# Attention and two mixer blocks on one core: float32 weight copies leave DRAM, Strassen sums are built from high and low parts, and the work gets a new order

## The chip, the cores and the metric

The kernel runs on one core of one Trainium2 chip. The metric is device time in microseconds (us) of one launch, lower is better. A core has a matrix engine (TensorE, PE in the profile, with its weight loads as PEld), a vector engine (DVE), a scalar engine (ACT), GpSimd (POOL) and an engine that issues DMA transfers (SP). Each runs its own queue of instructions in order and waits on semaphores.

## The reference, cut to what matters

```python
# q, k, v: (4, 12, 448, 64), float32; x: (4, 448, 768)
scores = cap * tanh((q @ k.T) / sqrt(64) / cap)
attn   = exp(scores - max); attn = attn / (sum(attn) + 1e-9)
x  = heads_to_columns(attn @ v)
# block 1
theta = x @ w_theta
y  = w_tok_r @ (x * cos(theta)) + w_tok_i @ (x * sin(theta))
u  = x + y
x  = u + relu(u @ w_ch)
# block 2
u  = x + (relu(x.T @ w_tok1) @ w_tok2).T
out = u + relu(u @ w_ch1) @ w_ch2          # 768 -> 1536 -> 768
```

All of it is float32. The kernel keeps that precision by splitting an operand into a high part in the float32r format and a low part (the rest), and adding three matmuls (high x high, high x low, low x high).

## The kernel before

**Stages.** The four batches are done as two pairs. First attention of all batches (`attn`), then, woven with the rest of attention, block 1 and block 2 of batches 0 and 1 (`token(0, ...)`, `rest(0)`), with plain products of 128 columns; then `token(1, ...)` and `rest(1)` for batches 2 and 3. For the second pair every product of block 1's theta, of `w_ch`, of `w_ch1` and of `w_ch2` is done by a Strassen-like scheme of seven products for eight (`fast`, `fast2`), two batches at a time. It needs, beside three quarters of a weight as they are, four sums of its quarters, `s1` to `s4`; they are made in `combine` and split again into high and low parts (tiles `F` in float32, `S` or `w` split).

**Weights.** Weights come in as float64, a pair of 32-bit words for each number (`raw`). `convert` builds the float32 value (`cw`) with ACT, DVE and POOL, splits it into `hl`, and writes the split to DRAM (`cu`, `ct`, `ca`, `cb`); for all weights of index 6 to 35 it also writes the float32 value itself to DRAM (`f6` to `f35`, dictionary `whole`). Where the second pair needs the sums, `combine` loads quarters of these float32 copies (`F<-f`); only for the first six weights it gets them by adding a high and a low part on DVE (`F<-w`). `RE`, `FE` and `SL` say which engine does which addition (v is DVE, p is POOL).

**Attention.** For each pair of heads and each chunk of keys, `scores` makes a matmul into a two-bank PSUM tile `sp`, ACT does tanh and exp into a tile `t` (three buffers, tag `t`; `tm` for the shared tail chunk), and `av` multiplies by the values. At the end of a pair of heads `finish` copies the result from PSUM to `xr` (two buffers), sends the sums through small DMAs (`pk`, `sr`, `dn`) to invert and spread them, multiplies `xr` by `dn`, and for batches 2 and 3 stores `xr` in DRAM (`xd`). A buffer of `xr` is free when that store has landed.

**Order.** All of this is recorded as operations and then put in order by a list scheduler (`Plan.schedule`). It takes the ready operation with the lowest priority number, and the table `RANKS` adds a shift to the priority of each operation. `SB` and `PS` give the number of buffers of each tag; a buffer is handed out in the order of recording.

Of the kernel before, what the change touches and what calls it, by code (L numbers as in the profile page):

```python
# [95 lines left out]
!s5aq>?{*P#S$S@yE250<wAIfxPFxoZfh7qTqJ}anuYKnbw0Z#gx?<yp=Hq!dQ}LaC-JK#Luhb&2(222aPF}X=H48_=*L4iUn7J@Q93-{C4~I+v6-
?R<iE~%MXw6spP?aKHIO#Y@mBs2wiF7XGX1rj9zwo3A?%{x>lv?hgAk_94B@4}LRk9_^>$KrGK9-dhww*M2wz+X;b@N#exXgicSBf}ZRJyrK*zZdj-3eM-
SZ(llNrKm86n(2xTI7F&mIloz=043(NDL7Av{c*!!4nK?`KAY@KnA;;tJ9msMG9h2utX<6K&6)3Sl+zTIv@jJ)3wnG<0H|M~;P1=#oUD6ytRz%%tABGa(f
DH-
s{LCys}3ZLLIN6m9B3`(w~Fmo`7r|8~CTP(Kq|E~39JN$N8G)ubzvevtI%)G5YyDf(RWPYC7H1m;*B+M3W;1?E(pzTc;O7W8ZmA@rUd!k9vd#7@e4QGOeB  # L100
-%2DB*;NyXpXqNO^}0aU7Ur^dZwL|X=TUEC@kFBMK4>8nWQ>xz5{ZkUvu43W;#T6*)G0*WhxUZ<3AELtpRJ5Lk+Sm4HKwl;q!%*oW#s=vUTMbb$-
dM$1PxIL^O?()v|B~_O8V-(J%mHh@dor%DMp<#i9~D0-
b0;n)alMR<4JE~J#JwBwdrRid2CyVNN*$Ej`okPhrYj=SMEe&9&3LowAP{B7{(~Z_gUJ{C2p5Lkyu9Dh&|}0_2O*RW4!y>hky94Oj-
ZKtSxJHp1E|S>~TVyf32^I^gECI*9h&H+g|csq`W6#D}6r6{Dwi(LTKtjn-WilkVT!IjPn!osYu>av>Ohcvss^4>E~1EUPil`wCh3L#hm-
=D67i++SBJq`tDDDF518OKq9e%dV4uD^=aFkwe3Q^(X4$9!n#xle>281(Rj?x<39Fd9R1xym`43hT5tN?PrZ@*IdjzgG7cew^&P@G{Ru6n=CVfY`ySHy8z
d5eF@9iO=F@&P;a$Slj5m?9((189BF~Nx?%vAxpPWV3Xdq)Z`cER!m$|)6of3>wc^hj^yAsT$HT0ijKJy9Z`R>fv!|1;Vw6x|dbfsMf#;ixWFEl(sXb#N-
nEOWhszm!M2|YMJ+ZnqcbL>O^|J@Qo-HqI9*6<|h`q1&*Zq{iR^ub>q<lOwgm>)6LE3`jNpM&Wm$;IhR+>yKg4)f?p{r;@QJ*;PCLSfp>pwCO0OK;ZnQOX
x_UT%WE>CoR8y0@^t^XYE^v>c$$leB-7@4nDikG3DFY*7fevhE$A>mtVMun8XU6YW^HkAH@DiEiqzg0}A&V-?}ht?6*>ckDBBzmz_^LQ6-
&2i&J87^@cdv;<|RIkUN-AwTQWit&pwPEGD=Ue=-1Wr;+7+Kwm8V?O(!cN1YSYy2j2sL344Fy`&7L#Z_(jG+H=zr%~xv7SrdhwRTm&Tw5qRcL&Nb=X-
rk=V-kX9=A+(@zoq$vLXW7-OL29OH~4{|fT+K-b@-  # L110
n^Crs@v3n~dXay+ZU_(1XV35HpEWr~S$WRqd}#lK?@i33Cv$5;+?aWOPCx&F)>52@afHLH=}zi)Sq8sm4ZqWUU|*^*)=SKxKjj1AeJ{W_hcMoygvQiaPk-
OiZYz9aDSfVho>IEY(6>r!N_;NU#x6&BNz#Yt^GV_sti@NfeUkX%Cfq6L?RvoO>^VX{#ymjS&N%%zXYW(5t<E^>JCyQ1(7k~0EPX9too<58lf)BQyAk9Sr
cNo^-@-fwow7BXO<%QHPmV#jl>CpW-
;D3A&{UYvk9L&^Z<GHZeIKE$D(Uv*?d5x<co})K33WspWd%4twJ2LoXhxsq8UGH_6<C{pDSMH44}E`6URC;efj*vv7T9!nmhuwheRIL)l#l+FQ-
2EUGK%m4XRtJNzdUbwk`v;m6Iq9C%&7_AgTz;#Hoo~AVGZ>*vsY7~aV_Z<)E`dWeC*vS`YA+zH|ngB--
>h*`sl^@HN>xIQw$o)=1n9t_cPF)i#>UmbYNa7`Z$|mcX=n{zDN7fgr4*_iM$(VJCO31*srC~-jy-VQLhqxFJ|lm;^&Na3w7?|thAu*8u;IC#;Hi#<Iu}B
3w8Le#rM8Fb}v65?_u)pqyFWzolO`>KiAN2amJp`cLCzfjC+*$8P>J(MTvygvkP^m(Dqa4+eleg@j=eeamuE02m5}FoMnzj;Cn47YY06fnd?btU&MG9==%
=RZ_+j|<wFPq=&vkg>xg?ZuP&J;3l0&clK%v4c1jjd_dd#QA^w3rPH+!K^L>yy6GapGDd_l`{d$e`ounTizZdPNO4cxs8<>aYvx+sik9b<1MB*pr@;dcz(
AXE*`g}^+$MoHov+*3|llguoHktap?t9vJOBd2V(*JqNYm(QTyIY(5G0^lldHrcy9U9Ih4NI*dd`9`L^tF`wqba`xI-
jG?P|}x^-jZd!X)QF}O&=@LCZDGg*GSuX&L>8sgcJ1lH0e9Z`;7Z?fHgTtn?LERDQ#9$=ZllZFA9(@$UZlTY|TF58#WMbR-  # L120
fd}p^pb*<JrK@1W-IwrQS`XE0BMkudnXhF24Vw-KE4o5kJJb4ZmRbegfxRGT|EPcBO6W$Y|WlHxM~IK^vfb7yymqSc~^aFQ8px$`A6riLjLL4|&~be;xJ5
(tn3+lP!`9<>|j9WtY(J<)mv;R+aIqksd()OSD-<_>s_`I$slBBcv&xL#W1{-B14oN!RBLoQ9Ui2*deq4?T#x!1W1;#*mB9g|-
c~|AcYWTg>;nti!d;P3Prv#;i|VnDy_hc4?bu1$g9I>UWK7ot_gdd~f6XBgT4*a7i$pSqqvTrk?|9N1fI>AJjwig(Bo5io*=;A^E*@hY9~BAgaQfgl@6j_
fHAm1j9|YlgF~;tTC!dPP;v{|BL)LNMA?4#fgh*9|>nQcgn|*zL{_WIx4dE8LaOb>OM#q2c4zp`)cyaLH8Y$UqhSUpmi974I=+dzEQ!#eDWHT?nwG$!Yul
{mOefuZvY{iFqQoBPWNWM#}OYUo=@E`Nxz>q%(Fa_F2{W$|9wIg!qfEiD<Q$T*baWx8Z6cMg|54ai|ahoM+Wgn^mEc!Z%FGL(r0_gDKh$y(IvL^tgib;3=
7M-Kd+NNn7Vtl&%Q1ivMt{~5_VDlJYgQ`HsTY(=Klxviczm1-
xK&Qk+%DGkiMQEzD@Us@FD@VHHTm9q0Rk#zr^>wgsVwEN$4vXOJ7|nFDu?lC_sMU*!WU?(x|fGGvddomzB1;oFyL2x9EF{&{}6BwmU7ls*v}q&NO2mOWS#
QM}3mMf%p^F@E_7+DSw!FAL9bS6J>pUPLQ`%ciZQ3f_m4IKZ$lDg%SAPMVo6W`<A?3#Q*BvQ3oiVD8~0!#A~UypYhVMos+{ln>yos_oD1Ftu=KgP`3=<W%
&M%vWntU<gX^wBkw42O#W+x-~0}v?uTQ1ZzW8QjrXc=-L2B32Z@)GzTjuEQQF#QF0-
<YKaMB;JL&O++@eXclf2IuAC?~qQRgn56+&0i2h(<@bT4{RuUuqjwjDC~g_DNK=aAQmbmV8N9OWxxo5ObE7oGO8$n4dOJBYEG5hm$=()K-  # L130
_f88hDal)_SNs?>ySCn*J>g<KiJhAbl-n11y7hOr+De~I!eKYm16Ca~qZN@6Y{(R2&H{}1Ob)@b&LR0FGk_;klMR-
# [1533 lines left out]
```

## Time and profile before

| what | value |
| --- | --- |
| median of three runs | 919.63 us (918.73 to 920.24) |
| the profiled execution, its own time | 919.92 us |
| its span, first to last instruction | 918.0 us |
| PE busy | 901.8 us (98%) |
| DVE busy | 686.2 us (75%) |
| ACT busy | 517.8 us (56%) |
| POOL busy | 350.2 us (38%) |
| DMA traffic | 169.25 MB, mean 184 GB/s |

The busy time of an engine is the union of its instructions. Matmuls overlap, so an uninterrupted PE shows as fully busy and the time that counts there is idle time and time at a lower granted clock. In a timeline row the bracket at the end is the idle time of that engine just before the row, with the instruction that ended it. [...]

### The profile page before, as it was taken

Reading aid. Unit: us, or ns where it says so; the run is one execution under the profiler, and the core shown is the slowest. Engines: PE = TensorE matmul, PEld = TensorE weight load, DVE = VectorE, ACT = ScalarE, POOL = GpSimd, SP = SyncE. Lnnn points to the kernel's source line nnn. Section 1 sums busy time; section 2 is a strip of 40 time slices with the busy share of each in tenths; the row PEclk is TensorE's granted clock in tenths of the full one; section 3 lists DMA queues with packets and bytes.
Section 4 is the critical chain, followed back from the end, with each engine's and each line's share of the span. In section 5 each row is a group of like instructions: output and inputs, shape, how many; then the busy total and the mean of one; then the engine's idle time right before and its main releaser. Section 6 shows DMA issues by size and latency. Waiting matters only on the chain.

```text
span 918.0 us, 13715 instructions
## 1 busy us (share of the span) xinstructions
PE 901.8 (98%) x4776; PEld 697.1 (76%) x4776; DVE 686.2 (75%) x1150; ACT 517.8 (56%) x871; POOL 350.2 (38%) x298
## 2 busy tenths in 40 slices
...
GB/s 220 225 241 235 261 216 250 180 270 175 167 126 201 263 252 85 168 217 173 286 268 236 214 277 193 382 148 78 52 124 135 55 30 102 95 193 101 220 116 143
DMA packets 97708, 169.25 MB, mean 184 GB/s; under 512 B 11752, under 2 KB 79976, under 8 KB 97640
## 3 DMA queue, kind: packets, MB, share of 16 engines
...
## 4 chain that ended last, share of the span: by engine, by line
PE 61%; DVE 4%; DMA 2%; ACT 2%; issue 1%; SPq 0%; POOL 0%; ACTq 0%; DVEq 0%; POOLq 0%
PE P L551 24%; PE c L551 18%; PE t L551 6%; PE tm L551 6%; PE wc L551 3%; PE av L551 2%; PE tp L551 1%; PE xp L551 1%; DMA raw<-wt 1%; DMA raw<-wu 1%; DMA pk<-sv 1%; PE sp L551 1%; ACT t L551 1%; DVE g L551 1%; DVE cw L551 0%
## 5 line engine op out<-in xcount | busy, mean ns | idle before, releaser
L551 POOL TENSOR_TENSOR cw<-cw,raw 128x384 uint32<-128x384 uint32 (+2 forms) x94 | 95.4, 1017 | 257.0 <-DVE cw L551 147.1
L551 PE MATMUL tm<-WT,zn 128*128 128x448 f32 x504 | 115.6, 376 | 0.2 <-DVE WT L551 0.2
L551 PEld LDWEIGHTS tm<-WT,zn 128*128 128x128 f32 x504 | 92.5, 189 | 18.5 <-issue 4.7
L551 ACT ACTIVATE t<-sp,consts 128x896 f32<-128x896 f32 x72 | 72.0, 1002 | 36.6 <-POOL t L551 12.1
L551 PE MATMUL c<-g,w 128*128 128x448 f32 x432 | 89.6, 365 | 0.1
L551 PE MATMUL c<-XHL,w 128*128 128x448 f32 x432 | 89.6, 366 | 0.0
L551 PEld LDWEIGHTS c<-XHL,w 128*128 128x128 f32 x432 | 81.0, 188 | 7.2
L551 PEld LDWEIGHTS c<-g,w 128*128 128x128 f32 x432 | 80.9, 188 | 7.1 <-DVE XT L551 0.5
L551 ACT ACTIVATE t<-t,consts 128x896 f32<-128x896 f32 x72 | 74.9, 1043 | 1.7
L551 PE MATMUL P<-XHL,w 128*128 128x448 f32 x324 | 72.9, 366 | 0.0
L551 POOL TENSOR_TENSOR F<-F,F 128x384 f32<-128x384 f32 (+1 forms) x42 | 43.0, 1023 | 76.7 <-DVE F L551 58.9
L551 POOL TENSOR_TENSOR t<-t,t 128x896 f32<-128x896 f32 x24 | 52.4, 2183 | 51.3 <-ACT t L551 13.6
L551 DVE SCALAR_TENSOR_TENSOR cw<-raw,cw 128x384 uint32<-128x384 uint32 (+2 forms) x94 | 69.7, 744 | 2.4
L551 ACT CAST w<-cw 128x384 fp32r<-128x384 f32 x72 | 35.2, 507 | 57.6 <-PE c L551 25.7
L551 PE MATMUL av<-t,vt 128*64 128x448 f32 x288 | 64.8, 556 | 2.6 <-ACT t L551 2.0
L551 PEld LDWEIGHTS P<-XHL,w 128*128 128x128 f32 x324 | 60.7, 188 | 5.3
L551 POOL TENSOR_TENSOR XHL<-XT,XHL 128x448 fp32r<-128x448 f32 x30 | 38.0, 1268 | 49.9 <-ACT XHL L551 30.0
L551 DVE TENSOR_TENSOR w<-cw,w 128x384 fp32r<-128x384 f32 x72 | 45.6, 645 | 13.4 <-ACT w L551 13.3
L551 PE MATMUL th<-XHL,w 128*128 128x448 f32 x216 | 52.1, 378 | 0.6 <-DVE rc L551 0.6
L551 ACT CAST S<-F 128x384 fp32r<-128x384 f32 (+1 forms) x72 | 31.5, 460 | 36.2 <-DVE F L551 16.9
L551 DVE TENSOR_SCALAR cw<-cw 128x384 uint32<-128x384 uint32 (+2 forms) x94 | 45.2, 481 | 8.3 <-ACT cw L551 7.4
L551 PEld LDWEIGHTS th<-XHL,w 128*128 128x128 f32 x216 | 38.6, 188 | 14.3 <-issue 8.6
...
## 6 DMA issues: line engine op xcount, KB each, us to landing
...
f<-cw SPq DMA_DIRECT2D x60, 192.0 KB
...
F<-f SPq DMA_DIRECT2D x36, 192.0 KB
...
```

Source lines behind the costliest of these rows:

```text
L551: getattr(eng[o.eng], name)(*map(real, a), **{x: real(y) for x, y in k.items()})
```

## The change

1. `convert` no longer writes float32 copies; the dictionary `whole`, the 60 stores `f<-cw` and the 72 loads `F<-f` are gone.
2. `combine` makes all four quarters by adding a high and a low part. For weights 6 to 11 and 12 to 23 these are 36 more additions on DVE (128x384); for weights 24 to 35 (`mixed2`) they are 18 on DVE and 18 on POOL (128x256, `RE["d"]` is `vpvp`). The quarter that was not loaded split before is loaded now: nine loads of a split weight are 128x1536 instead of 128x2x384, and 18 loads `S<-cu` of 128x256 are new.
3. `combine` no longer raises the priority of these operations.
4. `t` tiles rotate over five places: three buffers of tag `t` and two of tag `ex`, which stand empty until the second pair.
5. `xr` has three buffers instead of two.
6. `SHIFT`, the unused bytes that are put ahead of some tiles, and `RANKS` have new numbers. `GRP` is all ones, so the loop over chunks yields as before.

```diff
+TS = ("t","t","t","ex","ex")
-SB = {..., 't': 3, ..., 'xr': 2, ..., 'ex': 2}
+SB = {..., 't': 3, ..., 'xr': 3, ..., 'ex': 2}
-RE = "vvvv"
+RE = {"t":"vvvv","w":"vvvv","c":"vvvv","d":"vpvp"}
-SHIFT = {'w': 8, 'wg': 16, 'rc': 16}
+SHIFT = {'zx': 16, 'kq': 16, 'raw': 16, 't': 16, 'w': 16, 'wg': 16}
 RANKS = r"""
-c-lpq3D}KQ*T+w$SE5qNlp#b>84`+wqB1my5}}kLDPz...
+c-l3a2i%X<`^UdVgrt;Ji6rquN+b#uQW+(Yrj?M9EhH...
...
-        if key[0] == "u" and key[1] in plain:
-            if key[1] not in whole:
-                whole[key[1]] = dram(f"f{key[1]}", P, [DM])
-            sp_.dma_start(whole[key[1]][:, key[2] * n:(key[2] + 1) * n], wv)
...
     def quad(a, c):
-        return [("c", a, full(a)), ("c", c, half(c))]
+        return [("c", a, full(a)), ("c", c, full(c))]
...
+        def next_t():
+            tag = TS[count[0] % len(TS)]
+            count[0] += 1
+            return sbuf("t", tag, [1024])[...] if tag == "ex" else sbuf("t", tag, [2, S])
...
-                t = pt[c] = sbuf("t", "t", [2, S])
+                t = pt[c] = next_t()
...
-    def combine(t, srcs, N):
-        with pri(-100):
-            for j, src in zip((2, 0, 1, 3), srcs):
-                x[j] = sbuf("F", "cw", [CW])[:, :N]
-                if isinstance(src, tuple):
-                    (pool if RE[j] == "p" else dve).tensor_tensor(out=x[j], in0=f(src[0]), in1=f(src[1]), op=ALU.add)
-                else:
-                    sp_.dma_start(x[j], src)
+    def combine(t, srcs, N, how):
+        for j, src in zip((2, 0, 1, 3), srcs):
+            x[j] = sbuf("F", "cw", [CW])[:, :N]
+            (pool if how[j] == "p" else dve).tensor_tensor(out=x[j], in0=f(src[0]), in1=f(src[1]), op=ALU.add)
...
-        combine(t, [whole[24 + g * FB + q // 3][...] for q in (...)], N)
+        i, q = divmod(2 * (e + 3), 3)
+        weight("u", 24 + g * FB + i, None, DM // CW)
+        with pri(-100):
+            for h in range(2):
+                sp_.dma_start(f(t[0][h]), cache["u", 24 + g * FB + i][:, h, N * q:N * q + N])
+        combine(t, (t[0], A["22"], A["11"], A["12"]), N, RE["d"])
```

On each engine the number of instructions changes as follows: PE 4313 and 4313, with the same kinds and shapes; DVE 54 more; POOL 18 more; ACT two table loads more (22 instead of 20); SP 114 fewer (475 instead of 589). The order changes everywhere. Counting as one form the score matmuls, the float32 and the float32r ones apart, the `av` products (of `t` and of `tm` apart), the sums, the transposes and the 128-wide products, PE's order goes from one form to another 308 times before and 276 times now.

The first place is DVE in the token stage of the first pair, where results of attention of batch 2 go to `xr` (`xr_314`, `xr_330`, `xr_360` and `xr_384` are the first four, written in turn). Before, the third copy stands a little behind the conversion of `wt1`, ahead of work on the second buffer:

```order
L551 TENSOR_SCALAR cw_475_2225<-cw_475_2225 112x256
L551 TENSOR_SCALAR cw_472_2170<-cw_472_2170 112x256
L551 SCALAR_TENSOR_TENSOR cw_472_2170<-raw_438_2008,cw_472_2170 112x256
L551 COPY xr_360_2248<-av_341_1963 128x448
L551 SCALAR_TENSOR_TENSOR cw_475_2225<-raw_469_2080,cw_475_2225 112x256
L551 TENSOR_TENSOR rc_390_2218<-rc_390_2218,XT_82 128x448
L551 TENSOR_TENSOR xr_330_1900<-xr_330_1900,dn_333_2192 128x448
```

Now there is a third buffer, and it is the fourth copy that needs the place of `xr_314`; it stands 15 rows behind the multiplication that readies `xr_314` for its store:

```order
L559 TENSOR_TENSOR xr_314_1815<-xr_314_1815,dn_317_1942 128x448
L559 TENSOR_TENSOR rc_356_1994<-rc_356_1994,XT_82 128x448
L559 SCALAR_TENSOR_TENSOR pk_332_1888<-pk_332_1888,consts_74 56x16
L559 RECIPROCAL pk_332_1888<-pk_332_1888 56x16
L559 TENSOR_TENSOR rc_356_1994<-rc_356_1994,XT_82 128x448
L559 COPY sv_361_2056<-av_341_1903 128x448
L559 TENSOR_TENSOR zn_373_2060<-tp_374_2030,zn_372_2041 128x512
L559 COPY xr_360_2071<-av_341_1903 128x448
...
L559 TENSOR_SCALAR cw_470_2095<-cw_470_2095 128x384
L559 COPY xr_384_2124<-av_359_2045 128x448
```

The third copy no longer depends on the first store, and the fourth one does.

The second place is ACT a little later, where the last pieces of `wt2` (`raw_483`, then `raw_486`) are converted between tanh and exp of batch 3 (`t_498`, then `t_502`). Before, the last piece stands directly ahead of the tanh of `t_502`:

```order
L551 ACTIVATE cw_490_2779<-raw_483_2703 128x224
L551 CAST XHL_83<-XT_82 128x448
L551 CAST ch_488_2803<-cw_487_2742 128x224
L551 ACTIVATE cw_493_2825<-raw_486_2768 128x224
L551 ACTIVATE raw_486_2768<-raw_486_2768 128x224
L551 ACTIVATE t_502_2834<-sp_501_2818,consts_74 128x896
```

Now it stands directly ahead of the tanh of `t_498`, one chunk earlier, behind all the pieces before it:

```order
L559 ACTIVATE raw_483_2668<-raw_483_2668 128x224
L559 CAST XHL_83<-XT_82 128x448
L559 CAST ch_485_2749<-cw_484_2629 128x224
L559 CAST ch_488_2755<-cw_487_2706 128x224
L559 ACTIVATE raw_486_2715<-raw_486_2715 128x224
L559 ACTIVATE cw_493_2772<-raw_486_2715 128x224
L559 ACTIVATE t_498_2789<-sp_497_2774,consts_74 128x896
```

On SP the load of `raw_486` stands as the fifth row behind that of `raw_480`, where it was the 13th.

The third place is DVE at the very end, around the last `combine`. Before, its inputs are loaded and two additions of `F` stand between the additions to `XT`:

```order
L551 TENSOR_TENSOR XT_82<-P_1305_8411,XT_82 128x448
L551 TENSOR_TENSOR F_1323_8599<-F_1322_8592,F_1323_8599 128x256
L551 TENSOR_TENSOR F_1322_8592<-F_1324_8605,F_1322_8592 128x256
L551 TENSOR_TENSOR XT_82<-P_1307_8502,XT_82 128x448
L551 TENSOR_TENSOR S_1320_8640<-F_1323_8599,S_1320_8640 128x256
```

Now two quarters are added up there from their parts first (the other two on POOL):

```order
L559 TENSOR_TENSOR F_1322_8543<-S_1320_8139 128x256
L559 TENSOR_TENSOR F_1323_8550<-w_1308_8418 128x256
L559 TENSOR_TENSOR F_1323_8550<-F_1322_8543,F_1323_8550 128x256
L559 TENSOR_TENSOR XT_82<-P_1319_8525,XT_82 128x448
L559 TENSOR_TENSOR S_1320_8139<-F_1323_8550,S_1320_8139 128x256
L559 TENSOR_TENSOR F_1322_8543<-F_1324_8557,F_1322_8543 128x256
```

Each of the nine `mixed2` and nine late `weights4` has gained such rows.

## Rows read from the trace of the kernel before

**Rows 1.** The page, busy time of each engine: us, share of the span, instructions.
```profile
PE 901.8 (98%) x4776; PEld 697.1 (76%) x4776; DVE 686.2 (75%) x1150; ACT 517.8 (56%) x871; POOL 350.2 (38%) x298
```

**Rows 2.** Windows by stage: PE, PEld, DVE, ACT, POOL busy, clock, DMA, GB/s.
```profile
0.00:400.00 400.00, 388.83 (x2142) 225.55 (x2142) 303.14 (x546) 288.38 (x407) 141.80 (x112) 0.99 0.66 207
400.00:600.00 200.00, 199.86 (x989) 183.93 (x988) 137.12 (x230) 86.84 (x177) 64.35 (x56) 1.00 0.78 256
600.00:735.00 135.00, 133.95 (x736) 123.23 (x735) 106.36 (x157) 63.20 (x124) 58.91 (x49) 1.00 0.29 93
735.00:900.00 165.00, 164.72 (x846) 151.41 (x846) 129.07 (x201) 77.39 (x161) 80.40 (x76) 1.00 0.39 122
```

**Rows 3.** Timeline of PE, its longest waits: start, us, instructions, [idle before <-releaser].
```profile
34.99 0.97 PE L551 MATMUL av<-t,vt 128*64 128x448 f32 x4 [1.98 <-ACT t L551]
...
229.88 0.96 PE L551 MATMUL sp<-hl 64*128 64x448 f32 x6 [2.72 <-DVE xr L551]
...
291.97 1.77 PE L551 MATMUL av<-tm,vt 64*64 64x448 f32 x6 [2.21 <-ACT t L551]
...
607.02 0.66 PE L551 MATMUL tp<-ident,rc 128*128 128x128 f32 x4 [0.86 <-DVE rc L551]
```

**Rows 4.** Windows just behind the three longest waits; the clock follows POOL.
```profile
36.00:39.30 3.30, 3.30 (x18) 0.73 (x20) 2.73 (x6) 0.00 (x0) 1.34 (x2) 0.50 0.86 277
...
230.60:233.90 3.30, 3.30 (x12) 2.76 (x11) 1.65 (x4) 2.93 (x3) 1.76 (x1) 0.50 0.19 56
...
292.00:295.30 3.30, 3.30 (x10) 1.75 (x11) 2.70 (x6) 2.17 (x4) 1.89 (x2) 0.50 0.43 120
```

**Rows 5.** Timeline of SP and of DVE before the wait at 229.88.
```profile
221.27 0.46 SPq L551 DMA_DIRECT2D xd<-xr  x1
...
229.20 0.62 DVE L551 COPY xr<-av 128x448 f32<-128x448 f32 x1 [3.83 <-DMA xd<-xr]
```

**Rows 6.** Timeline of POOL, DVE and ACT before the wait at 34.99.
```profile
27.57 2.23 POOL L551 TENSOR_TENSOR t<-t,t 128x896 f32<-128x896 f32 x1 [3.03 <-ACT t L551]
27.77 2.25 DVE L551 TENSOR_SCALAR cw<-raw 128x384 f32<-128x384 f32 x1
...
32.13 0.51 ACT L551 CAST w<-cw 128x384 fp32r<-128x384 f32 x1 [0.94 <-POOL cw L551]
```

**Rows 7.** Timeline of SP and of ACT before the wait at 291.97.
```profile
281.78 0.46 SPq L551 DMA_DIRECT2D raw<-wt  x1
...
290.33 0.40 ACT L551 ACTIVATE cw<-raw 128x224 f32<-128x224 f32 x1 [5.20 <-DMA raw<-wt]
```

**Rows 8.** Additions: tile F (ns min/median/max); groups by form from 735 us.
```profile
L551 DVE TENSOR_TENSOR F<-w x12: 545/550/1199, 569.6 to 617.3; 128x384 f32<-128x384 f32 x12
...
L551 DVE TENSOR_TENSOR XT<-P,XT 128x448 f32<-128x448 f32 x63 | 38.2, 619 | 13.3 <-PE P L551 12.6
L551 DVE TENSOR_TENSOR g<-p,g 128x448 fp32r<-128x448 f32 x12 | 12.4, 1032 | 1.3 <-ACT g L551 1.2
...
L551 DVE TENSOR_TENSOR F<-F,F 128x256 f32<-128x256 f32 x18 | 9.4, 521 | 0.2
...
L551 POOL TENSOR_TENSOR F<-F,F 128x256 f32<-128x256 f32 x18 | 15.3, 850 | 25.9 <-DVE F L551 17.0 <-issue 7.9 <-POOL v L551 0.4
```

**Rows 9.** DMA issues of the page: count and KB of each.
```profile
f<-cw SPq DMA_DIRECT2D x60, 192.0 KB
...
F<-f SPq DMA_DIRECT2D x36, 192.0 KB
...
F<-f SPq DMA_DIRECT2D x36, 128.0 KB
```

**Rows 10.** Groups of instructions over the whole span: busy us, mean ns, idle before.
```profile
L551 PE MATMUL tm<-WT,zn 128*128 128x448 f32 x504 | 115.6, 376 | 0.2 <-DVE WT L551 0.2
...
L551 PE MATMUL c<-XHL,w 128*128 128x448 f32 x432 | 89.6, 366 | 0.0
...
L551 ACT ACT_TABLE_LOAD x20 | 25.7, 1283 | 6.5 <-PE sp L551 4.6 <-PE av L551 0.8 <-PEq L1658 0.7
```

More of the change, by code (lines that the diff above doesn't have):

```diff
@@ L101 @@
[L101 to L106, printed above, removed]
@@ new lines @@
+f-9q0kz-
+9r@R$xZ0K<~j@kHAOo&7~chE<pDIaP)+ZHO#4yep{&D1;IlLaY!Ghy)5G{WKLJX(*&G7DE~{pG2qP4eza$<wV6+0zV86%2I`IITXLKI{&3?$_HViI&Bmpy
+KlD{z!`TCVF7!=<5BAPx|4*8Zd-b^8CB?`C*7i-D*fp!ME9igrU-
+T8_e;9W%V{N8hfH77vpNBC{X6Scq$b^aT{1o`TIe7ZQBPF2WvH8dw9MRtG=||tjIpMvCbFV*wO*NTyz{!&D;*d2JSl^1w`)Dg<(4Y95Es=8r;K7OL6zFY_
+ky?TAii5i|ZI81qi?T!_Ew)J?hpq+tagKBOH0R`Y`D{~I8|WO)zGmscx!a5UKn~^M{P$%YyF$<G{f7H)zEx&kcaYD=F)m*YnFhW^@W3~Ww}-LH-WiE}!M^
+Q0XYUZ-f%krg-}1s=o%dl!K*t*PvK{ODHEYq5ws}Q3Pe*-
+>fU{W>{(b*H^FxnOJ`C^uL7xp5O#jRP=Qz%CO;TP`Df$d0Z^*ZCz<qMrWbres*Dh$;4_^h)P#XTp#=iBxVfv{jecA#$h<bwh3pXqVHwu{B&zW2=yw&u&Y@
@@ L217 @@
+m53;Vc@aho7_vSO%rBTu}6Jm?#`d5n>QKe8it-
+iNLj`|uZM>LYk>-5rt0J>dNG8;e69g|^J_&hxBs{%n!R>&&O<V*Bm==*QVZ__Ru<NMsTYTR+ZwE^LJLtkXB6pqX?9p6r9|k@pkmZh&lqj$zQM-yDyEA6Dq
+z5V~h^7V2%c-&Ysq{PZ|se7QuwHHL>q|7SkpQT=v_wtTF0cYKr-a$;vyWJND@A8;LIXNlJtqc3R`yfTZv0sJ_g^RSq;d*-ag4iwkQ$(*kNKaG8F#`q-
+^W7qrepP-
+qxN1$tQefa;R-LsFBj~KV#wJN?jUGF(qryk@ieMH}zg7erd^B?4sFJ{~b>y=2e_iXx&LNEW$v$=nxJz8)0qxPH1d(tdM|F6FnP+U%a?EeAZ*jf+
 """
@@ L829, in load_tok @@
         WS[2] = [w.rearrange("p (c o) -> p c o", o=S) for w in w2]
-    whole = {}
     def full(i):
@@ L842, in big @@
         units[j] = [t[:, 0], t[:, 1]]
-    def half(i):
-        return lambda j: big(j, i, [(DM // 2, DM // 2, DM // 2)])
     def fresh(i):
@@ L886, in attn_mix_kernel @@
         stream += [("c", (g, e), sixth(g, e)) for e in range(NC6 // 2)]
-    plain = set(range(6, 36))
     units = {}
@@ L918, in prep @@
             st[b, hp] = [vt, hl, kq, None, {}]
+        count = [0]
+        def next_t():
+            tag = TS[count[0] % len(TS)]
+            count[0] += 1
+            return sbuf("t", tag, [1024])[:, :2 * S].rearrange("p (a s) -> p a s", a=2) if tag == "ex" else sbuf("t", tag, [2, S])
         def rows(j):
@@ L1049, in attn @@
         todo = []
-        for b, hp, c in seq:
-            if c == 1 and hp % 2 == 0:
-                prep(*heads.pop(0))
-            scores(b, hp, c)
-            if c == 0 and heads:
-                prep(*heads.pop(0))
-            todo.append((b, hp, c))
-            while len(todo) > LAG:
-                av(*todo.pop(0))
-            yield 2.3
+        n = 0
+        while n < len(seq):
+            group = seq[n:n + GRP[seq[n][0]]]
+            n += len(group)
+            for b, hp, c in group:
+                if c == 1 and hp % 2 == 0:
+                    prep(*heads.pop(0))
+                scores(b, hp, c)
+                if c == 0 and heads:
+                    prep(*heads.pop(0))
+                todo.append((b, hp, c))
+            for _ in range(len(group)):
+                while len(todo) > LAG:
+                    av(*todo.pop(0))
+                yield 2.3
         while todo:
```

244 lines of the change are left out of this document (121 added, 123 removed).

## The prediction

> **What bounds the kernel now.** I read the page's busy times first: PE is busy for 901.8 of 918.0 us, and no other engine comes over 75% [rows 1]. The change leaves PE the same instructions. So time can come only from three places: from PE's idle time, from stretches in which its clock is low, and from the way its instructions follow each other. The windows by stage say where the idle time lies [rows 2]: 11.2 us of it before 400 us, 0.1 us from 400 to 600, 1.1 us from 600 to 735, 0.3 us from 735 to 900. The rest of the span is its end, with the last additions and stores. PE is thus held up in the stages with attention, and hardly at all where the Strassen sums are made.
>
> Next comes PE's timeline, for single waits [rows 3]. Three carry most of it: 1.98 us up to 34.99 for an exponential on ACT, 2.72 us up to 229.88 for a copy to `xr` on DVE, 2.21 us up to 291.97 for a tanh or exp. The fourth, 0.86 us at 607.02, is small. [...] At half the clock 3.3 us do the work of 1.65. So each of the three costs its wait and 1.65 us more: 3.63, 4.37 and 3.86 us, together 11.9 us. That is what this order can win back at most from long waits.
>
> Last I looked at what stood ahead of each. The wait at 229.88: DVE's third copy to `xr` sat 3.83 us for the store of the first (`xd<-xr`), which SP issued at 221.27 and which landed only about 229.2, some 8 us later [rows 5]. With two buffers the third copy needs the place of the first. The wait at 34.99: POOL ran an addition of 2.23 us, DVE's conversion beside it took 2.25 us, and so ACT's cast came late, with the exponential behind it in ACT's queue [rows 6]. The wait at 291.97: ACT sat 5.20 us for a piece of `wt2` that was issued at 281.78 and landed some 8.5 us later, and the tanh that PE needed stood behind it [rows 7].
>
> **The change part by part.** *Third buffer of `xr`.* The third copy no longer depends on the first store, so the 4.4 us at 229.88 go. What is late next is the fourth copy, which needs the first store now. In the new order 15 DVE rows lie between the multiplication ahead of that store and the fourth copy. Most of these are additions and copies of 128x384 to 128x448, of the size whose medians and means are 0.55 to 0.62 us [rows 8]; with the small ones about 8 us, against the 8 us of the store. It can still wait a little. Bounds: 0 and -4.4; I take -4.4.
>
> *Five places for exponentials.* A score no longer waits for one of three `t` tiles. This does not shorten ACT's queue, but the new order leaves more PE work between a score and its `av` in that stretch: counted in the program's order, each matmul at its usual spacing in the trace, at least 4.9 us where the tightest pair had 3.4. The wait at 34.99 was 1.98 us, so 1.5 us more would nearly cover it. Bounds 0 and -3.6; I take -3.6.
>
> *The pieces of `wt2`.* The last one stands ahead of an earlier tanh now, which is worse, but its load is issued 8 SP rows sooner, which is better: with the load 8.5 us long [rows 7] either could decide. Stores `f<-cw` that went ahead of such loads are gone, too. Bounds +1 and -3.9; I take -3.9, since the 60 stores of 192 KB and 72 loads of 192 and 128 KB were on the same queue [rows 9]: that is 11.5 MB out and as much back, of 169 MB, against 9 x 384 KB and 18 x 128 KB that are new (5.8 MB).
>
> *PE's order.* The form changes 276 instead of 308 times. In a stage with many changes a 128-wide matmul of `tm` takes 376 ns, in one with hardly any 366 ns [rows 10]; over 504 that is 5 us, and about twice as much if `th` and `wc`, 432 more, lose as much. A tenth fewer changes is worth 0.5 to 1 us; I take -1.0, between 0 and -3.
>
> *New waits in the first 400 us.* The whole order is new, and the order before had three long waits in it. An order with looser couplings will have fewer, but hardly none. I take one of the size of those before, 3.6 + 4.4 + 3.9 over three: +4.0. Bounds 0 and +11.9. Two more table loads on ACT are 2 x 1.28 us [rows 10]; ACT is busy 288 of 400 us there [rows 2], so they hide beside PE's work, and if they don't, they are part of this term.
>
> *The additions.* 36 on DVE at 0.55 us [rows 8], of which 16 (weights 6 to 11 and the first quad) come before 735 us, in a stage where DVE is busy 79%. From 735 on it is 20 of these and 18 of 128x256, which I price as the `F<-F` of that shape at 0.521 us: 11.0 + 9.4 = 20.4 us. The window has 129.07 of 165 us busy [rows 2]; with them 149.5, or 91%. POOL gets 18 x 0.850 = 15.3 us to its 80.4. PE's work hides all this as long as DVE keeps up, and today DVE waits for PE there: 12.6 us in front of the 63 additions `XT<-P` alone [rows 8]. At 91% bursts will now and then show: I take +1.0. Below it is bounded by 0, since these additions take nothing from any other engine. Above: at the longest mean of a kindred addition, 1.032 us, 38 cost 39.2 us and DVE has 168.3 us of work in 165, +3.3; if in addition half of POOL's 15.3 us hold DVE up, +7.6; together +10.9. The transfers that go were hidden: from 400 to 600, where DMA was busiest, PE lost 0.1 us.
>
> That last bound has a row for it: DVE's conversion that took 2.25 us lay beside a POOL addition of 2.23 us [rows 6]. [...]
>
> *The sum*, against the profiled execution's own 919.92 us (its span and 1.92 us around it): -4.4 - 3.6 - 3.9 - 1.0 + 4.0 + 1.0 = -7.9, so 912.0 us. The median of the runs shown is 919.63, 0.3 us lower, which is within their spread.
>
> **The rivals.** *No long wait at all:* the term of +4.0 is wrong and the small waits behind 600 us go too, 1.1 and 0.3 us [rows 2]: 912.0 - 4.0 - 1.4 = 906.6 us. For it speaks that all three causes are touched; against it, that ACT is still busy 72% of the first 400 us and DVE 76%, with an in-order queue each.
>
> *The waits only move:* three new ones for the three old, and what remains is the order's -1.0 and the additions' +1.0: 919.9 us, no change. For it speaks that none of the three waits follows from the amount of work; such waits come from how queues happen to line up, and the scheduler that made both orders is the same. Against it speaks the wait for `xr`, which has a cause in the code.
>
> *DVE becomes the bound of the last stage.* Its place is 735 us to the end, its price the +10.9 above in place of +1.0, its time 912.0 + 9.9 = 921.9 us, slower than before. It decides from a price of 8.9 us on, which eats all the other terms. For it speak the 91% and rows 6; against it, that PE has products to spare there (it lost 0.3 us of 165 with DVE at 78%), and that the additions may be placed wherever DVE is free.
>
> **How the numbers follow.** What a measurement of this kernel can tell from no change is about 0.2%, or 1.8 us. Chances: the forecast 0.52 (its own range, one wait more or less, 908 to 916); no long wait 0.20; the waits only move 0.15; DVE as bound 0.13. Faster than 917.8 us: 0.52 + 0.20 + 0.03 of the third = 0.75. Within 0.2%: 0.09 of the third and 0.02 of the last = 0.11. Slower: 0.03 and 0.11 = 0.14. The range reaches from a little under the first rival, 905.5, to the second, 920.0, and leaves out the slow rival and the better end of the first.
>
> **What would show it.** In the profile of the changed kernel: no wait of PE for DVE's `xr` over 1 us; the granted clock at 0.5 in one stretch before 400 us, not in three; PE idle of some 6 to 7 us instead of 11.2 before 400 us; PE idle from 735 to 900 us still under 1.5 us with DVE at 88 to 93%; added `F<-w` of 128x384 at 0.55 to 0.85 us on DVE. The prediction is wrong if two or more low stretches of the clock remain, or if PE waits for DVE or POOL by more than 4 us behind 600 us.

## The result, and the profile after

The changed kernel takes 903.57 us in the median (902.85 to 904.83, 4 runs), the kernel before 919.93 us beside it: a ratio of 0.982, 95% interval 0.980 to 0.984. The forecast was 912.0 us, with a range from 905.5. The sign was right, the gain is twice the forecast, and the time lies 1.9 us under the range. The profiled execution is one of 903.56 us.

The page's busy times and the windows by stage, in the columns of [rows 1, 2]:

```profile
PE 887.3 (98%) x4776; PEld 695.6 (77%) x4776; DVE 713.2 (79%) x1204; ACT 520.4 (58%) x873; POOL 372.3 (41%) x316
```

```profile
0.00:400.00 400.00, 393.39 (x2230) 240.57 (x2231) 310.20 (x563) 296.15 (x417) 144.00 (x113) 1.00 0.64 203
400.00:600.00 200.00, 200.00 (x1000) 185.40 (x1000) 147.39 (x243) 92.86 (x192) 75.17 (x64) 1.00 0.66 216
600.00:735.00 135.00, 134.98 (x778) 125.95 (x777) 111.75 (x168) 60.39 (x120) 56.86 (x46) 1.00 0.19 63
735.00:900.00 165.00, 158.98 (x773) 143.64 (x771) 143.81 (x232) 70.95 (x147) 96.24 (x94) 1.00 0.34 110
```

PE is idle for 6.6 us instead of 11.2 before 400 us, and for 0.02 instead of 1.05 us from 600 to 735. From 735 on it loses more than before; of the 6.0 us there 1.7 lie behind its last matmul, which ends at 898.3, so 4.3 are waits. But PE is also busy for 14.5 us less, with the same 4776 instructions. The low clock that is gone (below) explains 5.1 of it, no wait can explain the rest, and the forecast's sum had 1.0 for it.

PE's timeline, all waits of over 0.5 us behind the first microseconds; the last entry is the idle time before and what ended it:

```profile
52.25 0.98 PE L559 MATMUL av<-tm,vt 64*64 64x448 f32 x8 [0.63 <-ACT tm L559]
...
64.26 1.02 PE L559 MATMUL sp<-kq 64*128 64x448 f32 x4 [0.55 <-ACT t L559]
...
75.27 1.02 PE L559 MATMUL sm<-sv,spread 128*128 128x448 f32 x2 [0.91 <-DVE sv L559]
...
282.40 0.98 PE L559 MATMUL av<-tm,vt 64*64 64x448 f32 x6 [0.74 <-ACT t L559]
...
392.04 8.15 PE L559 MATMUL c<-XHL,w 128*128 128x448 f32 x39 [1.42 <-DVE XHL L559]
...
736.87 1.08 PE L559 MATMUL t<-W,h 128*128 128x448 f32 x4 [0.57 <-DVE h L559]
...
822.21 0.47 PE L559 MATMUL P<-g,w 128*128 128x448 f32 x1 [1.33 <-ACT g L559]
...
873.58 0.47 PE L559 MATMUL P<-g,S 128*128 128x448 f32 x1 [1.20 <-POOL S L559]
```

The three long waits of [rows 3] are gone, the longest new one is 1.42 us, and no low stretch of the clock follows any of them, where there were three [rows 4]; the granted clock is 1.00, full speed, in all four windows.

The groups of matmuls, over the whole span:

```profile
L559 PE MATMUL tm<-WT,zn 128*128 128x448 f32 x504 | 111.4, 370 | 0.0
...
L559 PE MATMUL c<-XHL,w 128*128 128x448 f32 x432 | 88.8, 364 | 1.4 <-DVE XHL L559 1.4
...
L559 PE MATMUL th<-XHL,w 128*128 128x448 f32 x216 | 49.0, 371 | 0.0
...
L559 PE MATMUL wc<-XHL,w 128*128 128x448 f32 x216 | 46.5, 368 | 0.0
...
L559 PE MATMUL t<-xn,W 112*128 112x256 f32 x288 | 36.5, 282 | 0.0
```

`tm` falls from 376 to 370 ns, and `c<-XHL`, which has hardly any change of form near it, from 366 to 364 [rows 10]. That hints at two causes: one that belongs to stages with changes of form, and one for all matmuls.

Where the 16.4 us came from can be added up from the two traces. I took the start of each matmul and of the next, subtracted the idle time and half of each low stretch, and summed what is left by the form of the matmul:

| part | before | after | difference |
|---|---|---|---|
| low clock (three stretches of 3.41 us at 0.50) | 5.1 | 0.0 | -5.1 |
| PE idle before 400 us, between matmuls | 9.7 | 5.1 | -4.5 |
| PE idle, 400 to 735 us | 1.2 | 0.0 | -1.2 |
| PE idle from 735 us to its last matmul | 0.3 | 4.3 | +4.0 |
| spacing of matmuls without waits | 896.3 | 887.0 | -9.3 |
| sum | | | -16.1 |

The 5.1 is an estimate from the clock of 0.50. In two of the three stretches the trace has 128-row matmuls of 448 columns behind each other, 373 to 374 ns from start to start, where the median outside is 204; by that the row would be 4.6, and the spacing's -9.8.

The experiments divide the -9.3, and ask who owns the +4.0. In six profiles with the changed kernel's order on PE and its addresses, and without a low stretch, the spacing lies between 886.3 and 887.7 us, so a difference of about 1 us in that row means nothing.

### The profile page after: what moved, and what is told of

Read it like the earlier page. It is cut to its first block, busy times and chain, and to the rows that moved or that the text cites. A ratio compares the mean times of both kernels' runs of the same rounds, so it can differ in the third digit from the quotient of the medians.

```text
span 901.8 us, 13508 instructions
## 1 busy us (share of the span) xinstructions
PE 887.3 (98%) x4776; PEld 695.6 (77%) x4776; DVE 713.2 (79%) x1204; ACT 520.4 (58%) x873; POOL 372.3 (41%) x316
## 4 chain that ended last, share of the span: by engine, by line
PE 83%; DVE 9%; ACT 3%; DMA 2%; POOL 2%; issue 1%; SPq 0%; POOLq 0%; ACTq 0%; DVEq 0%
PE P L559 20%; PE c L559 19%; PE tm L559 12%; PE av L559 7%; PE sp L559 6%; PE th L559 5%; PE t L559 5%; PE wc L559 4%; PE tp L559 2%; PE sm L559 2%; DVE cw L559 1%; DVE XT L559 1%; ACT t L559 1%; PE xp L559 1%; DMA raw<-wu 1%
## 5 line engine op out<-in xcount | busy, mean ns | idle before, releaser
L559 PE MATMUL tm<-WT,zn 128*128 128x448 f32 x504 | 111.4, 370 | 0.0
L559 DVE SCALAR_TENSOR_TENSOR cw<-raw,cw 128x384 uint32<-128x384 uint32 (+2 forms) x94 | 62.3, 667 | 2.4
L559 DVE TENSOR_SCALAR cw<-cw 128x384 uint32<-128x384 uint32 (+2 forms) x94 | 50.6, 541 | 8.3 <-ACT cw L559 7.8
L559 PE MATMUL P<-g,S 128*128 128x448 f32 x216 | 48.1, 366 | 1.7 <-POOL S L559 1.2
L559 PE MATMUL P<-T,S 128*128 128x448 f32 x216 | 49.0, 366 | 0.4 <-DVE T L559 0.2
```

The costliest lines, as they stand in the source:

```text
L559: getattr(eng[o.eng], name)(*map(real, a), **{x: real(y) for x, y in k.items()})
```

## The experiments

### The pads: four kernels

Each edit is one line. With the changed kernel's order and the pads of before:

```diff
-SHIFT = {'zx': 16, 'kq': 16, 'raw': 16, 't': 16, 'w': 16, 'wg': 16}
+SHIFT = {'w': 8, 'wg': 16, 'rc': 16}
```

> The changed kernel, every engine's order as it is, with the pads of the kernel before in place of the new ones. With the new pads all moving operands and weights of the float32r matmuls begin at multiples of 64 B; with these, 1638 of 3582 moving operands and 2709 of 3582 weights begin at 32 B past one. Theory P (the pads are what the forecast left out): the 128-wide matmuls, 201 ns from one start to the next in the changed kernel, go back towards the 205 ns of before; over some 2,900 of them +4 to +6 us, so 907.5 to 909.5 us against 903.6. Rival O (the new order of PE, with fewer changes of form, won all of it): 903 to 904.5 us.

Measured: 908.24 us (908.16 to 908.34). The pads are worth 4.7 us against 903.57, and theory P holds. In the trace the spacing without waits is 4.1 us longer. The groups part the two causes: `c<-XHL` is back at the 366 ns of before, while `tm` keeps nearly all that it won (371, where it had 376 before):

```profile
L559 PE MATMUL tm<-WT,zn 128*128 128x448 f32 x504 | 112.1, 371 | 0.0
...
L559 PE MATMUL c<-XHL,w 128*128 128x448 f32 x432 | 89.6, 366 | 1.8 <-DVE XHL L559 1.8
```

The same line the other way round, in the kernel before:

> The kernel before, every engine's order as it was, with the new pads alone: all operands of the float32r matmuls begin at multiples of 64 B. Theory P: 914 to 916 us against 919.9, the start-to-start time of the 128-wide matmuls at 201 to 203 ns, and the three low stretches of the clock still there. Rival O: 919 to 920.5 us, 205 ns. A third case: faster matmuls that only reach the same three waits sooner, so that part of the gain is lost in longer waits, 916 to 918 us.

Measured: 917.82 us, ratio 0.998 (0.996 to 0.999), which is 2.4 us less. Its spacing is 2.1 us shorter, while the waits of 2.75 and 2.18 us and their low stretches are still there (the first long wait is 1.41 us in this run, without a low stretch). So little was lost to the waits; the same pads simply did half as much in this kernel. That speaks against the reason I had in mind, that all operands begin at multiples of 64 B now.

With the start address of each operand (as the program was given it in SBUF) beside the trace's start times, another order appears. What sorts the spacings is the distance of the start of a matmul's moving operand from the start of weights, modulo 128 B; I counted it to the weights of the *next* matmul. Mean ns from start to start, with the number of pairs (128 rows, 448 columns, spacings of 190 to 215 ns):

| kernel | 0 | 32 | 64 | 96 | 256 columns, mostly |
|---|---|---|---|---|---|
| before | 203.1 (291) | 203.9 (65) | 202.3 (753) | 204.2 (1763) | 119.7, at 96 |
| changed | 203.1 (375) | | 202.2 (2546) | | 115.5, at 64 |
| changed, pads of before | 203.2 (340) | 203.3 (73) | 202.3 (726) | 204.2 (1782) | 119.7, at 96 |
| before, new pads | 203.3 (886) | | 202.2 (1981) | | 119.5, at 0 |

Whether the next matmul's weights count or the matmul's own is not shown: in the changed kernel the two distances are the same in all but 69 of 2,922 pairs. Of these, 40 with the own weights at 64 and the next ones at 0 take 202.1 ns, and 26 the other way round 204.0, which in this kernel speaks rather for the own.

The new pads put fewer pairs at 64 in the kernel before than in the changed one, and its 256-column matmuls not at all. Two more kernels, both the changed one, part the two explanations. The first puts 32 B in front of everything in SBUF:

```diff
+    con.tile([P, 8], F32, name="first")
     sb = ctx.enter_context(tc.tile_pool(name="sb", bufs=1))
```

> The changed kernel with 32 B more in front of everything in SBUF: now all operands of the float32r matmuls begin 32 B past a multiple of 64 B, and the distance between the start of a moving operand and that of the next matmul's weights is what it was (64 B modulo 128 in 2636 of 3228 pairs, 0 in 592). Theory R (the distance of the two starts modulo 128 B sets the spacing; in the traces so far 202.2 ns at 64, 203.2 at 0, 204.2 at 32 or 96): 903 to 904.5 us, spacing as before. Rival A (being at a multiple of 64 B does it): 907 to 909 us.

The second leaves out one pad:

```diff
-SHIFT = {'zx': 16, 'kq': 16, 'raw': 16, 't': 16, 'w': 16, 'wg': 16}
+SHIFT = {'zx': 16, 'kq': 16, 'raw': 16, 'w': 16, 'wg': 16}
```

> The changed kernel without the pad of t alone: all operands still begin at multiples of 64 B, but the distance of the two starts modulo 128 B is 0 in 2284 pairs (592 in the changed kernel) and also in the 284 pairs of 256 columns. Theory R: 1692 x 1.0 ns + 284 x 4 ns = +2.8 us, so 906 to 907 us, and 119.5 instead of 115 ns in the 256-column matmuls. Rival A (multiples of 64 B): 903 to 904.5 us.

Measured, with the changed kernel beside them on the same chip at 904.12 us: 905.32 us with all operands moved by 32 B, 908.60 us with the one pad gone. In the first trace the spacing is what it was (202.2 ns at 64 in 2547 pairs, 115.5 ns in 256 columns; 634.9 us for all 128-row matmuls in both); its 1.2 us lie in waits. In the second there are 2013 pairs at 0, with 204.0 ns, and the 256 columns take 119.6. Group lines of the second:

```profile
L559 PE MATMUL c<-XHL,w 128*128 128x448 f32 x432 | 90.2, 368 | 1.3 <-DVE XHL L559 1.3
...
L559 PE MATMUL t<-xn,W 112*128 112x256 f32 x288 | 37.7, 286 | 0.0
```

`c<-XHL` went from 364 to 368 ns and `t<-xn` from 282 to 286 by leaving out 64 B. So theory R stands and rival A falls: multiples of 64 B do nothing, the distance does. Its size was too small in the forecast of this run: +2.8 was said, the spacing grew by 3.5 us against the changed kernel beside it (4.3 against the first profile), the time by 4.5. A distance of 0 cost 1 ns in the kernels before it and 2 ns here, and most of that is one stage: `c<-XHL`, which has at most one pair at 0 in the other kernels of the table, takes 205.6 ns there (429 pairs), all others together 203.5 (1,584 pairs). Why that stage pays more stays open.

### The slots: xr and the exponentials

In the kernel before, one line each, every engine's order kept:

```diff
-            return sb.tile([P, *free], dt, name=n, tag=tag, bufs=SB[tag])
+            return sb.tile([P, *free], dt, name=n, tag=tag, bufs=3 if tag == "xr" else SB[tag])
```

> The kernel before in its own order, with a third buffer for xr as the only edit. The forecast's term: the wait of PE at 229.88 us (2.72) and the low clock behind it (1.65) go, 915.5 us. Rival (what is late next takes its place, a store or another engine): 917 to 920 us, a wait of PE of over 1 us remains near 230 us.

Measured: 914.78 us, ratio 0.995 (0.993 to 0.996): -5.4 us where -4.4 was forecast. Its waits at 34.86 and 286.67 us (1.50 and 2.11) remain, the one of 2.72 us for `xr` is gone, and a smaller one of 0.88 us has come:

```profile
34.86 0.97 PE L551 MATMUL av<-t,vt 128*64 128x448 f32 x4 [1.50 <-ACT t L551]
...
252.16 0.86 PE L551 MATMUL sp<-hl 64*128 64x448 f32 x6 [0.88 <-DVE xr L551]
...
286.67 1.64 PE L551 MATMUL av<-tm,vt 64*64 64x448 f32 x6 [2.11 <-ACT t L551]
```

The 1.0 us beyond the forecast need not be `xr`'s: in the profiled run the first of the other waits is 0.5 us shorter and no low stretch of the clock follows it.

```diff
+            if name == "t" and tag == "t":
+                count[0] += 1
+                if TS[(count[0] - 1) % 5] == "ex":
+                    return sb.tile([P, 1024], dt, name=n, tag="ex", bufs=2)[:, :2 * S].rearrange("p (a s) -> p a s", a=2)
```

> The kernel before in its own order, with the exponentials in five places in turn (three t, two ex) as the only edit. The forecast said that five places pay through an order with more PE work between a score and its av, so with the order kept: 919.4 to 920.4 us, the wait at 34.99 us still there. Rival (the place itself was what the exponential waited for): the wait of 1.98 us and its 1.65 us of low clock go, 916.3 us.

Measured: 919.77 us, ratio 1.000 (0.999 to 1.001), with a wait of 2.03 us at 34.98. Five places alone are worth nothing; the forecast had said that they pay through an order with more PE work in between. No run shows that: the new order without the third buffer or without the five places was not tried, so the order alone may have removed the wait at 34.99.

The third buffer and the new pads together:

> The kernel before in its own order with two edits: a third buffer for xr, and the new pads. If the two add up: -5.4 (measured alone) and -4.7 (the pads as measured in the changed kernel) give 910 us; with the pads at what they gave alone in the kernel before, -2.4, 912.4 us. Rival (the faster matmuls lose what they win in the two long waits left, at 35 and 292 us): 913 to 915 us. What lies between this and 903.6 us is then the order's: the two other long waits, the fewer changes of form, less the late waits.

Measured: 913.59 us (911.72 to 914.30). The median is worse than either sum, and where the rival had it; but the runs spread over the second sum, 912.4, too, so they don't part the two. What is left to 903.57 us is the order's, with the five places that it uses. PE's timeline shows that two long waits of before are still there:

```profile
35.27 0.97 PE L551 MATMUL av<-t,vt 128*64 128x448 f32 x4 [1.98 <-ACT t L551]
...
287.32 0.98 PE L551 MATMUL av<-tm,vt 64*64 64x448 f32 x6 [2.44 <-ACT t L551]
```

### The stores

In the kernel before, the 60 stores left out and the loads pointed elsewhere:

```diff
             sp_.dma_start(whole[key[1]][:, key[2] * n:(key[2] + 1) * n], wv)
+            plan.ops[-1].calls = []
...
                     sp_.dma_start(x[j], src)
+                    i = next(i for i in whole if whole[i].buf is src.buf)
+                    plan.ops[-1].calls = [("dma_start", (x[j], cache["u", i][:, 0].then(src.path[-1])), {})]
```

> The kernel before in its own order without its 60 stores of weights to DRAM; the loads that read them read as many bytes of the high parts' copy instead, so the Strassen sums leave out the low parts. Theory (in the order of before these transfers are hidden, as the forecast had it): 919 to 920.5 us, the three long waits and low stretches as they were. Rival (they held places or queues that PE waited for in the end): 917 us or less.

Measured: 920.79 against 920.87 us, ratio 1.001 (1.000 to 1.002). In the order of before the stores cost nothing. In the new order:

```diff
+        if name == "u" and i >= 6:
+            if i not in whole:
+                whole[i] = dram(f"f{i}", P, [DM])
+            more[plan.ops[-1].n] = whole[i][:, j * n:(j + 1) * n], wv
```

> The changed kernel with the 60 stores of weights to DRAM put back, each issued right behind the operation that ends its weight; nothing reads them. Theory (the transfers that went were hidden, as the forecast had it): 903 to 904.5 us. Rival (their 11.5 MB held up the loads that PE waits for): 905 us or more, with new waits of PE for a load or for a weight's slot before 735 us.

Measured: 916.15 us, +12.6 us. I had not expected that. The waits of ACT from 400 to 520 us (total, times, longest):

```profile
ACT cw L559 <- DMA f<-cw: 50.4, 20, 4.4
ACT w L559 <- PE c L559: 14.8, 8, 4.5
```

and the window of that stage, with the DMA share of 0.78 that it had before the change [rows 2]:

```profile
400.00:600.00 200.00, 193.24 (x939) 176.70 (x938) 134.63 (x225) 86.86 (x179) 67.17 (x59) 0.98 0.78 250
```

ACT cannot begin the next conversion until a store has landed and given back one of the four places of `cw`; 20 such waits add up to 50.4 us. PE is idle for 6.8 of the 200 us, and for 6.8 us more its clock is at half. Is it the bytes or the place? The last line of the edit with another source tells:

```diff
-            more[plan.ops[-1].n] = whole[i][:, j * n:(j + 1) * n], wv
+            more[plan.ops[-1].n] = whole[i][:, j * n:(j + 1) * n], f(hl[:, 0])
```

> The changed kernel with 60 stores of the same size at the same points of the queue as in the run with the stores put back, but read from the high parts in w, which another store reads as well, in place of cw. Theory C (there it was the four places of cw, each held until its store had landed, that held up the conversions): 903.5 to 906 us. Rival (the bytes or the queue of SP): 913 us or more, as with the stores from cw.

Measured: 902.86 us (902.77 to 904.15). Theory C holds:

```profile
400.00:600.00 200.00, 200.00 (x1001) 185.41 (x1000) 147.49 (x244) 93.08 (x192) 75.02 (x65) 1.00 0.75 255
```

As many bytes go out (a DMA share of 0.75), and PE does not lose a thing. ACT waits for one of these stores once:

```profile
ACT w L559 <- DMA f<-w: 1.3, 1, 1.3
```

### PE's order

In the changed kernel the finished order is edited: where two groups of a narrow form stand next to each other on PE, the next group of 128-row matmuls whose inputs are already there is put between them (12 places).

```diff
-        order = self.plan()
+        order = spread(self.plan(), SPREAD)
```

> The changed kernel with the order of PE alone edited: in 12 places a 128-row matmul group is put between two neighbours of a narrower form, so the form changes 300 times in place of 276; the kernel before has 308. Theory F (a change between a 128-row and a narrower form costs about 0.09 us, which was read from the spacings on either side of changes: 297 ns into one, 287 ns out of one, where 201 to 205 are usual): 24 x 0.09 = +2.2 us, 905.5 to 906 us. Rival (the changes cost nothing of their own, as the next weight load hides them): 903 to 904 us. If PE's idle time changes, that part is taken off first.

Measured: 924.47 us, +20.9 us, and no test of its theory: it counted the 112-row matmuls `t<-xn` as a narrow form, so beside the 12 places it split that stage in 45 more, and PE waited there for DVE's `xn`, with two low stretches of 3.41 us behind:

```profile
PE t L605 <- DVE xn L605: 4.7, 3, 2.3
```

I repeated it with these left alone.

> The changed kernel with PE's order alone edited, as in the run before this one, but only at matmuls of 64 rows or columns: in 12 places a group of three 128-row matmuls goes between two neighbours of a narrower form; no 112-row matmul is moved. Theory F: 24 more changes at 0.09 us, +2.2 us of spacing without waits; with no new wait 905.5 to 906 us. Rival: the spacing stays and the time is 903 to 904 us. New waits of PE are taken off before the comparison.

Measured: 910.42 us (908.03 to 911.25), +6.9 us against the changed kernel's first runs (+6.3 against its later ones, which were on another chip). Idle time grew by 1.6 us, the spacing without waits by 5.2 us, more than twice theory F. PE's timeline of one place, first the changed kernel, then the edited one (start, duration, group):

```profile
100.35 1.72 PE L559 MATMUL av<-t,vt 128*64 128x448 f32 x8
102.01 1.48 PE L559 MATMUL th<-XHL,w 128*128 128x448 f32 x6
103.33 0.60 PE L559 MATMUL tp<-ident,rc 128*128 128x128 f32 x4
```

```profile
100.04 0.97 PE L605 MATMUL av<-t,vt 128*64 128x448 f32 x4
100.94 0.88 PE L605 MATMUL th<-XHL,w 128*128 128x448 f32 x3
101.75 0.97 PE L605 MATMUL av<-t,vt 128*64 128x448 f32 x4
102.65 0.88 PE L605 MATMUL th<-XHL,w 128*128 128x448 f32 x3
103.37 0.60 PE L605 MATMUL tp<-ident,rc 128*128 128x128 f32 x4
```

The same 14 matmuls take 103.33 - 100.35 = 2.98 us in one, 103.37 - 100.04 = 3.33 us in the other. One more visit of the narrow form thus costs 0.35 us here, and 5.2/12 = 0.44 us in the mean. The single starts show where: about 0.09 us into it, 0.09 out of it, 0.1 at the first 128-row matmul behind it, and 0.04 in the first pair of `av`. Theory F had the first two alone.

### The late waits

In the changed kernel the additions of high and low parts from weight 6 on are left out (72 instructions):

```diff
+        if late_w:
+            h = {j: f(src[0]) for j, src in zip((2, 0, 1, 3), srcs)}
+            for o in plan.ops[-8:-4]:
+                o.calls = []
```

> The changed kernel, every engine's order as it is, without the 72 additions of high and low parts from weight 6 on (54 on DVE, 18 on POOL): the Strassen sums read the high parts directly, so the low parts of these weights are left out of the sums. Theory L (the 4.3 us of PE's idle time from 735 to 900 us are the price of these additions): idle there falls under 1.5 us, as before the change, and the time to 899.5 to 901 us from 903.6. Rival (the waits come from the new order, not from the work on DVE and POOL): idle stays at 3 to 4.5 us, 903 to 904 us.

Measured: 901.02 us (898.88 to 902.57), -2.5 us, and between the two theories. The windows show DVE at 123.25 instead of 143.81 of 165 us, and yet PE's waits remain to the greater part:

```profile
735.00:900.00 165.00, 159.61 (x779) 145.03 (x778) 123.25 (x199) 69.76 (x148) 80.88 (x77) 1.00 0.34 111
```

```profile
822.27 0.47 PE L559 MATMUL P<-g,w 128*128 128x448 f32 x1 [1.05 <-ACT g L559]
...
875.43 2.48 PE L559 MATMUL P<-g,w 128*128 128x448 f32 x11 [0.56 <-DVE g L559]
```

Idle time from 735 us to the last matmul falls from 4.3 to 2.7 us. About 1.6 us of it are the additions'; the other 2.7 are there without them. Most of that I put down to the order, since the kernel before lost 0.3 us there, but no run shows it.

Three small moves in the finished order:

```diff
+    for x in (dve[i + 2], dve[i + 3]):
+        earlier(x, pk)
+    for x in (pool[j - 1], pool[j - 2]):
+        later(x, v)
+    f.eng = "DVE"
```

> The changed kernel with three small moves, all work kept: on DVE the addition XT<-t and the conversion XHL behind it go ahead of two 56x16 operations that waited 3.28 us for a load (at 390 us); on POOL the addition v<-v,p goes ahead of two S<-F,S (at 816 us); one addition F<-F of 128x256 goes from POOL to DVE (at 869 us). Theory W (the waits of 1.42, 1.33 and 1.20 us are the order's, each from one engine's queue): they shrink by 1.4, 1.0 and 0.9 us, 900 to 901 us. Rival (DVE and POOL have too much work there, the wait comes back close by): 903 to 904 us.

Measured: 902.85 us (901.58 to 903.20), 0.7 us under the 903.57 of the changed kernel, which is less than their runs spread. The first move worked. The two late ones only moved the wait: PE stands 1.17 us for POOL's `S` at 818.47 instead of 1.33 for `g` at 822.21, and 0.90 us for `g` at 875.17 instead of 1.20 at 873.58. So the first move by itself, with the changed kernel beside it:

> The changed kernel with the one move of DVE alone (XT<-t and XHL ahead of the two 56x16 operations that wait for a load at 390 us), all work kept. If the wait of 1.42 us is that queue's: -1.3 us against the changed kernel run beside it, about 902.2 us. Rival (PE reaches its next wait sooner and gives it back): no difference.

> The changed kernel itself, once more, as the mark for the three runs beside it: 903 to 904 us.

Measured: 902.28 us (901.74 to 903.53) against 904.12 us (902.81 to 904.51). The wait at 392 us is gone, and PE's idle time behind it is as before (4.6 us from 600 us on, 4.7 in the run beside it). Not all of the 1.8 us is its doing: in all, PE is idle for only 0.6 us less, as a wait at 282 us is longer in this run (1.30 us), and the spacing is 1.4 us shorter, which is no more than it varies by from run to run. What DVE did there, in the changed kernel and with the move:

```profile
390.01 0.23 DVE L559 SCALAR_TENSOR_TENSOR pk<-pk,consts 56x16 f32<-56x16 f32 x1 [3.28 <-DMA pk<-sv]
390.27 0.25 DVE L559 RECIPROCAL pk<-pk 56x16 f32<-56x16 f32 x1
390.44 0.55 DVE L559 TENSOR_TENSOR XT<-t,XT 128x448 f32<-128x448 f32 x1
390.92 1.07 DVE L559 TENSOR_TENSOR XHL<-XT,XHL 128x896 fp32r<-128x896 f32 x1
```

```profile
387.53 1.08 DVE L581 TENSOR_TENSOR XHL<-XT,XHL 128x896 fp32r<-128x896 f32 x1
...
389.77 0.23 DVE L581 SCALAR_TENSOR_TENSOR pk<-pk,consts 56x16 f32<-56x16 f32 x1 [1.16 <-DMA pk<-sv]
```

A 56x16 operation stood 3.28 us in front of the conversion that PE needed. This version has the lowest median of those here that do all the work; it clearly beats the kernel before (0.981, 0.979 to 0.983), and the changed kernel by 1.8 us, with intervals that still touch.

## Why the prediction was wrong in size

Its terms, in its own order, beside what was measured:

| term | forecast | measured | by |
|---|---|---|---|
| third buffer of `xr` | -4.4 | -4.4 | the wait at 229.88 and its low stretch gone; alone, -5.4 in the median |
| five exponential places | -3.6 | -3.6 | the wait at 34.99 and its low stretch gone; the places without the order, 0 |
| pieces of `wt2` | -3.9 | -3.9 | the wait at 291.97 and its low stretch gone; not run alone |
| PE's order, form changes | -1.0 (0 to -3) | about -5.2 | spacing -9.3 less the pads' -4.1 |
| new waits before 400 us | +4.0 | +2.4 | idle 9.7 - 6.9 (three waits) leaves 2.8, found 5.1 |
| additions, late waits | +1.0 | +4.0 | idle from 735 us |
| waits from 400 to 735 us | 0 | -1.2 | windows |
| pads | not priced | -4.1 to -4.7 | pads put back |

In the first three rows the size is that of a wait that is gone in the changed kernel; that the named part of the change removed it was shown for `xr` alone. The three rows from new waits down come to +5.2, where +5.0 was forecast: their errors happened to cancel.

**The step that failed first** is the opening sentence that "the change leaves PE the same instructions", so that time could come only from idle time, the clock, and the way instructions follow each other. The new pads stood in the diff, and the sum has no term for them. They change the operands' addresses, and with them the spacing of some 1,800 matmuls by about 2 ns and of 288 by 4 ns. That alone takes the forecast from 912.0 to some 907.5, inside its range.

**The second** is the step "a tenth fewer changes is worth 0.5 to 1 us; I take -1.0". It was mis-sized fivefold. It read the price from the means of the 128-row groups alone [rows 10], and so missed what a visit costs the narrow form itself; and it took the count of all changes (308 to 276), where the visits from a 128-row form to a narrow one fell by far more, from 53 to 37 (the four into the 112-row form counted). Sixteen visits at 0.35 to 0.44 us are 5.6 to 7.0 us; in the traces the changes among narrow forms rose from 99 to 108, and what these took back no run shows. With the pads of before in both kernels, 3.3 of the 5.2 us lie in the spacing of 128-row matmuls and 1.9 in the rest. The runs show the price of a visit, 0.35 us at one place and 0.44 us in the mean of twelve; what it pays for they don't show.

**The new waits** came as forecast, PE idle for 6.6 us in the first 400 us where "some 6 to 7" was said. But none was followed by a low stretch of the clock, where the forecast allowed for one. Neither of the two signs that it named for being wrong appeared (two low stretches; over 4 us of waits for DVE or POOL behind 600 us, where they are 2.9): they watched the waits, and most of what failed was the spacing.

**The additions** were about rightly sized as work: `F<-w` of 128x384 took 586 ns in the last stage, 550 had been taken, and DVE is at 87% of the window, a little under the 88 to 93 that had been said.

```profile
L559 DVE TENSOR_TENSOR F<-w 128x384 f32<-128x384 f32 x16 | 8.6, 586 | 0.8 <-POOL S L559 0.8
...
L559 DVE TENSOR_TENSOR F<-S 128x256 f32<-128x256 f32 x9 | 5.6, 618 | 0.0
```

What was wrong is "PE idle from 735 to 900 us still under 1.5 us". It is 4.3 us. By the run without the additions 1.6 are theirs; the rest is there without them, probably by the order. The bound of +10.9 was not reached. That half of POOL's 15.3 us would hold DVE up, as it assumes, no run shows. What the trace of the changed kernel shows is that the long ones among these additions lie beside POOL rows. Of the 48 `F<-w` of 128x384 over the whole span, 38 have no addition or other `TENSOR_TENSOR` of POOL beside them and took 544 to 558 ns; the other ten took 547 to 1519, six of them 960 or more. The nine `F<-S` of 128x256 take 618 ns in the mean, 415 in the median: five without such a row 410 to 415, four with one 602 to 975. `XT<-P`, which has an input in PSUM, shows nothing of the kind, 607 to 627 ns in 49 cases with such a row and 611 to 627 in 14 without. The row that the forecast named for its bound [rows 6] is not an addition but a conversion `cw<-raw` with one tensor as input; of these, in 128x384, six took 344 to 367 ns alone and six 344 to 2255 beside POOL.

**The transfers** were hidden, as the forecast had it, but for a narrower reason than it gave. Their bytes cost nothing in either order (920.79 against 920.87 us without them in the old one, 902.86 against 903.57 with them, from `w`, in the new one). Their hold on the places of `cw` costs nothing in the old order and 12.6 us in the new one. The price of an edit thus depends on the order it is put into.

Of the rivals, "no long wait at all" at 906.6 us came nearest. Half of its condition held: no long wait and no low stretch before 400 us. The other half, that the small waits go too, did not (+2.4 and +4.0 us), and what brought the time below it was in no rival either, the spacing. The waits did not only move, and DVE did not become the bound: PE is still busy for 98% of the span.
